# Giving a hand-ordered FFN block to a list scheduler: sigmoid attention and a squared-ReLU FFN on one core

## The chip, the core and the metric

The kernel runs on one core of a Trainium2 chip. The time is the device time of one execution in microseconds (us). The engines are TensorE (PE, with its weight loads shown apart as PEld), VectorE (DVE), ScalarE (ACT), GpSimd (POOL) and SyncE (SP), which issues nearly all transfers. Each engine works through its own instructions in program order and waits for the others by semaphores.

## The reference, cut to what matters

```python
batch, n_heads, seq, head_dim = (8, 12, 448, 64)
n_tokens, d_model, d_ff = (3584, 768, 2048)
...
scores = scale * np.matmul(q, k.transpose(0, 1, 3, 2)) - np.log(S)
attn = 1.0 / (1.0 + np.exp(-scores))
np.matmul(attn, v)
...
h = x @ w_in
r = np.maximum(h, 0.0)
g = s * (r * r) + b
g @ w_out
```

The attention's output, laid out as tokens x 768, is `x`. All inputs are float32; the weights reach the chip as int64 words of doubles and are turned into float32 there.

## The kernel before, in words

**Stages.** The attention runs over 24 quads of heads and stores `x` to DRAM (`xd`). While it runs, DVE and ACT turn the weights into float32 tiles `wf` (one per layer and chunk f of 128 of the 2048 middle features, so 16 chunks per layer). Then comes the *plain block*: token block 0 (512 tokens) goes through the FFN in the ordinary way. The other six token blocks follow in two groups of three by a fast bilinear scheme, whose products need sums of weight blocks. Those sums (`t_0_f_g` for layer 0) are made during the plain block.

**Numbers.** Every operand is split into a rounded part and a remainder (hi on ACT by `copy`, lo on DVE by `sub`), and a product takes three matmuls: hi*hi, hi*lo, lo*hi.

**The plain block.** For each of the 16 chunks, in the order 0, 8, 1, 9, ..., 7, 15:

- `ffn1` (line 804): 18 matmuls into `ph` with the split weight tile `w_0_f`;
- `activate` (line 1262): Relu, Square, Identity, copy on ACT and one subtraction on DVE make `g_f`;
- `ffn2` (line 1272): 18 matmuls into six banks `po` with `w_1_f` and `g_f`. It runs one chunk behind, so PE does ffn1(1), ffn2(0), ffn1(2), ffn2(1), ...; I call each of the 32 pieces of 18 matmuls a *half*.

Beside that, ACT and DVE split each weight tile (`base`, line 546), SP stores the split tile to DRAM (`wd`), from where the products will fetch it (`wu`), and DVE makes the sums `t_0_f_g` (25 additions per f, seven tiles), which are rounded on ACT, subtracted on DVE and stored by SP as well. Two chunks (7 and 15 of layer 0) are still turned into float32 here. Near the end SP loads tokens (`a`) and the first fetched weights (`wu`).

**Where tiles lie.** `w_0_f` and the tiles `t` come from the slots `cx`: eight tiles "c", and five tiles "t" that lie where the attention's buffers were. A slot is free again when its store has landed. `w_1_f` has three buffers (`p2`) and `g` three.

**What sets the order.** In the plain block before, the loop at line 1301 writes the instructions in the order of its statements: per chunk the rounding of the next chunk's weights, half a share of the sums, the activation, the other weight tile, the rest of the share (`rows_until`). Once a queue holds an instruction that has to wait, all behind it wait. The products behind the block are ordered by a list scheduler, class `Planner` (line 247): every operation gets an engine, a duration, what it needs, and a latest time; the scheduler keeps a clock per engine, always issues the operation that can start first, and among several the one that is due first; PE's order is fixed. After the block the scheduler has its own clock set anew, and that code is the same in both kernels.

In the tables below L811 is `ffn1`, L1276 `ffn2`, L543 the rounding of a weight tile, L1265 to L1268 the activation, L487 the rounding of a sum tile, L414 and L417 every addition and subtraction on DVE, L531 and L555 the stores to `wd`, L913 the fetch of `wu`, and L1004 and L1013 the products.

Of the kernel before, what the change touches and what calls it, by code (L numbers as in the profile page):

```python
# [325 lines left out]
def sigmoid_attention_relu2_ffn(  # L326
# [36 lines left out]
    class Slots:  # L363
# [182 lines left out]
    def base(l, f, t=None):  # L546

        t = t or base_hi(l, f)
        sub(t[:, :, 1], wf[l][f], f32(t[:, :, 0]))
# [712 lines left out]
    def activate(f, ph):  # L1262
        g = gp.tile([P, 2, TB], F32R, tag="g", name=f"g_{f}")
        r = rt.tile([P, TB], F32, tag="r", name=f"r_{f}")
        nc.scalar.activation(r, ph, AF.Relu)  # L1265
# [2 lines left out]
        nc.scalar.copy(g[:, 0], r)  # L1268
# [140 lines left out]
```

## Time and profile before

| | before |
|---|---|
| median of 3 runs | 1035.58 us (1034.74 to 1035.64) |
| the profiled execution | 1035.62 us, its span 1033.8 us |
| PE busy | 1018.3 us (98%) |
| DVE, ACT busy | 882.9 us (85%), 716.4 us (69%) |
| plain block on PE | 250.75 to 395.94 us of the span |

The span is the time from the first to the last instruction. PE is busy 98% of it, so only its few gaps and slow stretches can be gained. Rows of the timeline give start, duration, engine, line, output<-input, count, and in brackets the idle time of that engine before the row with what ended it. Names in such rows leave out buffer numbers.

### The profile page before, as it was taken

The page shows a single profiled execution, that of the slowest core. Times are in us where ns is not written, and L with a number is a line of the kernel's source. Part 1 is how long each engine was busy: PE and PEld are TensorE (multiplying, and loading weights), DVE is VectorE, ACT ScalarE, POOL GpSimd, SP SyncE. Part 2 cuts the span into 40 slices and gives each one's busy share as a digit, 9 for nine tenths or more (in the row PEclk, how much of TensorE's full clock was granted, in tenths as well). Part 3 has the DMA queues.
Part 4 walks back from the last instruction along what each step waited for, and adds up shares of the span by engine and source line. Part 5 has one row for each costly group of instructions (what it writes and reads, how often), then busy time and mean ns, then how long its engine had stood idle before and what let it go on. Part 6 is the DMA issues. An engine that isn't in the chain of part 4 may idle for free.

```text
span 1033.8 us, 13813 instructions
## 1 busy us (share of the span) xinstructions
PE 1018.3 (98%) x5194; PEld 761.5 (74%) x5194; DVE 882.9 (85%) x989; ACT 716.4 (69%) x772; POOL 0.2 (0%) x4
## 2 busy tenths in 40 slices
PE   9999999998999999999999999999999999999998
PEld 4545455554776787887887888888888887888887
DVE  6889898997887865999988999899768668999997
ACT  7889998997667656665899964523655889965421
POOL 0000000000000000000000000000000000000000
PEclk9999999999999999999999999999999999999999
DMA  8788999896898899898876666699776666666675
GB/s 335 270 301 303 337 337 387 308 379 233 312 356 295 316 333 401 325 362 303 272 248 186 194 192 196 211 356 311 237 215 195 192 196 190 187 200 188 214 227 185
DMA packets 101073, 278.77 MB, mean 270 GB/s; under 512 B 10000, under 2 KB 23184, under 8 KB 101008
## 3 DMA queue, kind: packets, MB, share of 16 engines
q1 hardware_dynamic: 100720, 277.45, 78.4%
q8 instruction: 41, 0.67, 0.3%
q10 hardware_dynamic: 288, 0.46, 0.1%
q14 instruction: 24, 0.20, 0.1%
HBM read 193.99 MB, written 83.89 MB: 269 GB/s over the span
## 4 chain that ended last, share of the span: by engine, by line
PE 78%; DVE 11%; ACT 5%; DMA 4%; issue 3%; SPq 0%; DVEq 0%; ACTq 0%
PE b L1013 30%; PE b L1004 22%; PE pav L685 10%; PE psc L651 8%; DVE t L417 3%; PE ph L811 2%; PE psc_l L672 2%; PE pav L694 2%; PE po L1276 2%; DVE w L417 1%; DVE r L414 1%; DVE t L414 1%; ACT t L487 1%; ACT w L543 1%; DMA wr<-wr 1%
## 5 line engine op out<-in xcount | busy, mean ns | idle before, releaser
L1004 PE MATMUL b<-o_0h,wu 128*128 128x512 f32 x928 | 287.1, 390 | 0.8 <-DVE r L417 0.7
L1004 PEld LDWEIGHTS b<-o_0h,wu 128*128 128x128 f32 x928 | 174.2, 188 | 38.6 <-DVE r L417 1.6
L1004 PE MATMUL b<-o_0l,wu 128*128 128x512 f32 x464 | 180.8, 390 | 1.0 <-DVE o_0l L417 1.0
L1013 PE MATMUL b<-o_0h,wu 128*128 128x512 f32 x464 | 152.4, 389 | 0.0
L1013 PE MATMUL b<-o_1h,wu 128*128 128x512 f32 x456 | 149.7, 389 | 0.0
L631 ACT ACTIVATE a<-psc,nls 128x896 f32<-128x896 f32 x144 | 132.8, 1009 | 12.2 <-PE psc L651 10.6
L685 PE MATMUL pav<-a,v 128*64 128x448 f32 x576 | 113.8, 543 | 0.0
L414 DVE TENSOR_TENSOR r<-r,b 128x1024 f32<-128x1024 f32 x74 | 89.4, 1218 | 27.1 <-PE b L1004 17.9
L417 DVE TENSOR_TENSOR r<-r,b 128x1024 f32<-128x1024 f32 x66 | 80.2, 1218 | 25.2 <-PE b L1004 16.5
L1004 PEld LDWEIGHTS b<-o_0l,wu 128*128 128x128 f32 x464 | 87.1, 188 | 19.6 <-DVE o_0l L417 1.9
L1013 PEld LDWEIGHTS b<-o_0h,wu 128*128 128x128 f32 x464 | 87.1, 188 | 18.3 <-ACT r L1059 0.3
L1013 PEld LDWEIGHTS b<-o_1h,wu 128*128 128x128 f32 x456 | 85.6, 188 | 17.8
L1013 PE MATMUL b<-o_0l,wu 128*128 128x512 f32 x232 | 90.3, 389 | 0.0
L1013 PE MATMUL b<-o_1l,wu 128*128 128x512 f32 x228 | 88.7, 389 | 0.0
L685 PEld LDWEIGHTS pav<-a,v 128*64 128x64 f32 x576 | 39.1, 137 | 63.8 <-issue 45.1
L487 ACT CAST t<-t 128x768 fp32r<-128x768 f32 (+2 forms) x62 | 44.3, 730 | 53.2 <-DVE t L417 39.3
L954 ACT CAST o_0h<-r 128x1024 fp32r<-128x1024 f32 x26 | 27.1, 1051 | 67.9 <-DVE r L417 40.0
L811 PE MATMUL ph<-x0h,w 128*128 128x512 f32 x192 | 64.5, 404 | 9.1 <-ACT w L543 5.6
L1276 PE MATMUL po<-g,w 128*128 128x512 f32 x288 | 67.7, 389 | 0.0
L1059 ACT ACTIVATE r<-b 128x1024 f32<-128x1024 f32 x46 | 46.4, 1026 | 28.5 <-DVE r L414 13.8
L1276 PEld LDWEIGHTS po<-g,w 128*128 128x128 f32 x288 | 54.1, 188 | 11.2
L417 DVE TENSOR_TENSOR t<-t 128x768 fp32r<-128x768 f32 (+2 forms) x70 | 53.9, 779 | 9.1 <-ACT t L487 8.2
(115 smaller groups left out, 1701.6 us busy)
## 6 DMA issues: line engine op xcount, KB each, us to landing
wu<-wd SPq DMA_DIRECT2D x232, 512.0 KB, 3.6
wd<-t SPq DMA_DIRECT2D x36, 768.0 KB, 4.7
qk<-qk_t SPq DMA_DIRECT2D x23, 896.0 KB, 6.5
st<-w_out SPq DMA_DIRECT2D x16, 768.0 KB, 8.8
st<-w_in SPq DMA_DIRECT2D x16, 768.0 KB, 8.8
wd<-t SPq DMA_DIRECT2D x22, 512.0 KB, 5.4
v<-v_t SPq DMA_DIRECT2D x24, 448.0 KB, 5.2
xd<-xo SPq DMA_DIRECT2D x24, 448.0 KB, 3.4
```

Of the source, the lines that this page charges most:

```text
L414: nc.vector.tensor_tensor(o, x, y, op=ALU.add)
L417: nc.vector.tensor_tensor(o, x, y, op=ALU.subtract)
L487: nc.scalar.copy(ts[g][:, :n, 0], f32(ts[g][:, :n, 1]))
L631: nc.scalar.activation(a, psc[:, :, :S], AF.Sigmoid, bias=nls, scale=SCALE)
L651: nc.tensor.matmul(o[:, j, :S], two[wi][r, i, cols], two[xi][r, i, :S], start=m == 0, stop=m == 2,)
L685: nc.tensor.matmul(pav[r, i, :S], ld_[1][:, 3 * i + c, j, :], a[i, c][:, j, :], start=c == 0, stop=False,)
L811: nc.tensor.matmul(ph, w[:, k, wi, kc * P : (kc + 1) * P], x0[h][xi][:, cc, :], start=m == 0, stop=m == 3 * NCC - 1,)
L954: nc.scalar.copy(hi.t, v.t)
L1004: nc.tensor.matmul(bk[:, j], wt[:, j, wi, c * P : (c + 1) * P], tiles[xi][:, c, :], start=first and m == 0, stop=m == 3 * KC - 1, skip_gro ...
L1013: nc.tensor.matmul(bk[:, e], wt[:, f, wi, e * P : (e + 1) * P], tiles[gi][:, f], start=first and f == 0 and m == 0, stop=p == np_ - 1 and ...
L1059: nc.scalar.activation(v.t, bank_t[b], AF.Copy, scale=-1.0)
L1276: nc.tensor.matmul(pos[e], w[:, k, wi, kc * P : (kc + 1) * P], g[:, gi, :], start=first and i == 0, stop=last and i == 2,)
```

## The change

The loop of the plain block is replaced by operations for a second `Planner` (`plan1`): each half on PE, each rounding, subtraction, activation, each single addition of the weight sums, each store, the two late conversions, the token loads and the first fetches. Each has a duration, needs and a due time. The work left over from the attention (three subtractions and three stores of `t_1_1_g`) becomes such an operation too, instead of coming first. The five "t" slots now come ahead of the free "c" slots. What is computed and how many instructions there are is the same: the instruction lists of both kernels count 3052 rows on PE, 991 on DVE, 776 on ACT and 512 on SP. PE's instructions stand in the same order; those of the attention and of the products keep theirs too.

```diff
-LATE, LATE_AT, LATE_FOR = 2, 2, 4
-ROWS_FOR = 3.5
-TOKENS = (5, 6, 8, 8)
+LATE = 2
+ROWS_DUE = ((10.0, 44.0), (40.0, 72.0), (68.0, 98.0), (90.0, 120.0))
+CONV_DUE = (50.0, 70.0)
+OPEN_DUE = 98.0
+TOKENS = 8
+AHEAD_1, AHEAD_R = 16.0, 40.0
 SUMS_FROM, SUMS_TO = (4, 10), 24
 LATER_SUMS = (2, 3)
 LATER_DUE = ((30.0, 84.0), (86.0, 140.0))
...
-        def more(self, pl, n, tag, when=-99.0):
-            self.free_ += [(when, pl, f"{tag}{i}") for i in range(n)]
+        def more(self, pl, n, tag, when=-99.0, front=False):
+            new = [(when, pl, f"{tag}{i}") for i in range(n)]
+            self.free_ = new + self.free_ if front else self.free_ + new
...
-    ticks(NL, "DVE")
-    for fn in stores:
-        fn()
-    w1 = w1[0]
-    ph0 = ffn1(order[0], w1)
+    ph0 = ffn1(order[0], w1[0])
+    cx.free(w1[0])
     at.close()
...
-    cx.more(pool(blk, "t2", 1), 5, "t")
+    cx.more(pool(blk, "t2", 1), 5, "t", front=True)
...
-    def activate(f, ph):
-        g = gp.tile([P, 2, TB], F32R, tag="g", name=f"g_{f}")
-        r = rt.tile([P, TB], F32, tag="r", name=f"r_{f}")
-        nc.scalar.activation(r, ph, AF.Relu)
-        nc.scalar.activation(r, r, AF.Square)
-        nc.scalar.activation(r, r, AF.Identity, bias=b_sb, scale=s_sb)
-        nc.scalar.copy(g[:, 0], r)
-        sub(g[:, 1], r, f32(g[:, 0]))
-        return g
...
-    held = None
-    w2 = {}
-    row_jobs = [
...
-    cost = sum(j[1] for j in row_jobs[0])
-    before = LATE_AT + LATE * LATE_FOR
-    shares = [(NQ4 - 1) * cost / before] * before + [cost / ROWS_FOR] * (NF - before)
-    row_jobs = collections.deque(j for q_ in row_jobs for j in q_)
-    spent = due = 0.0
-
-    def rows_until(x, roundings=True):
...
+    plan1 = Planner(cx)
+    HALF = 4.09
+    w_t, w_lo, g_t, acts, ffns, ph_t = {}, {}, {}, {}, {}, {0: ph0}
+    row_op, readers, nearly = {}, [], []
+
+    def due(i, l):
+        return max(0.0, (2 * i - 1 + 2 * l) * HALF)
+
+    def weights(l, i):
+        f = order[i]
+        uses = [2 - l]
+
+        def drop(at):
+            uses[0] -= 1
+            if not uses[0]:
+                cx.free(w_t[l, i], at)
+
+        def run_hi(at):
+            w_t[l, i] = base_hi(l, f)
+
+        def keep(at):
+            base_store(l, f, w_t[l, i])
+            if not l:
+                drop(at + 5.0)
+
+        h = plan1.op("ACT", 0.76, [ffns.get((1, i - 3))] if l else [], run_hi, 1 - l, early=AHEAD_1)
+        d = plan1.op("DVE", 0.89, [h], lambda at: base_lo(l, f, w_t[l, i]))
+        k = plan1.op("SP", 0.64 * len(base_rows(l, f)[0]), [d], keep, lag=4.0, late=due(i, l) + 10.0)
+        for r in base_rows(l, f)[0]:
+            row_op[l, r, f % NQ4] = k
+        if f % NP < NP - 1:
...
+    ffns[0, 0] = plan1.op("PE", HALF, [], lambda at: None, late=0.0)
+
+    def first_ffn(i):
+        d, drop = w_lo[0, i]
+
+        def run(at):
+            ph_t[i] = ffn1(order[i], w_t[0, i])
+            drop(at)
+
+        ffns[0, i] = plan1.op("PE", HALF, [d, acts.get(i - 2)], run, late=due(i, 0))
+
+    def second_ffn(i):
+        def run(at):
+            ffn2(w_t[1, i], g_t[i], i == 0, False)
+
+        ffns[1, i] = plan1.op("PE", HALF, [w_lo[1, i][0], g_lo[i]], run, late=due(i, 1))
+
+    g_lo = {}
+
+    def activation(i):
+        f = order[i]
+
+        def run(at):
+            g = g_t[i] = gp.tile([P, 2, TB], F32R, tag="g", name=f"g_{f}")
+            r = r_t[i] = rt.tile([P, TB], F32, tag="r", name=f"r_{f}")
+            nc.scalar.activation(r, ph_t[i], AF.Relu)
+            nc.scalar.activation(r, r, AF.Square)
+            nc.scalar.activation(r, r, AF.Identity, bias=b_sb, scale=s_sb)
+            nc.scalar.copy(g[:, 0], r)
+
+        a = acts[i] = plan1.op("ACT", 2.7, [ffns.get((0, i)), ffns.get((1, i - 3))], run, late=due(i, 1) - 3.6)
+        g_lo[i] = plan1.op("DVE", 0.68, [a], lambda at: sub(g_t[i][:, 1], r_t[i], f32(g_t[i][:, 0])))
...
+    def weight_sums(f):
...
+        chain = [conv.get(f + NP - NQ4), conv.get(f + NF - NQ4)]
...
+        for kind, time, g, fn in jobs:
...
+                his[g] = plan1.op("ACT", 0.04 + 0.24 * len(names[g]), chain, lambda at, fn=fn: fn())
...
+                def run(at, fn=fn, first=tuple(fresh)):
...
+                o = plan1.op("DVE", 0.36, chain, run, len(fresh), early=AHEAD_R)
...
+                o = plan1.op("DVE", time, [his[g]] + chain, lambda at, fn=fn: fn())
...
+                k = plan1.op("SP", 0.64 * len(names[g]), [o], keep, lag=4.0, late=a + (b - a) * spent / total)
...
+    for k, x in enumerate(late):
+        late_conversion(k, *x)
+    for i in range(NF):
+        weights(1, i)
+        if i:
+            weights(0, i)
+            first_ffn(i)
+        activation(i)
+        if i:
+            second_ffn(i - 1)
+    for f in range(NQ4):
+        weight_sums(f)
+
...
+    o = plan1.op("SP", 0.0, readers, opened, late=OPEN_DUE)
+    for k in range(len(FIRST_LOADS)):
+        if k < TOKENS:
+            plan1.op("SP", 1.28, [o], lambda at, k=k: start(FIRST_LOADS[k : k + 1]), late=OPEN_DUE + 2.8 * k)
+    x = None
+    for k in range(AHEAD):
+        _, l, row, p = stream[k]
+        after = [o, x] + [row_op.get((l, row, f)) for f in (2 * p, 2 * p + 1)]
+        x = plan1.op("SP", 1.28, after, lambda at: fetch(), late=OPEN_DUE + 6.0 + 2.8 * k)
+
+    def left(at):
+        ticks(NL, "DVE")
+        for fn in stores:
             fn()
-            spent += w
-
-    for i, f in enumerate(order):
-        if i > NF - 4:
-            a, b = TOKENS[i + 3 - NF : i + 5 - NF]
-            start(FIRST_LOADS[a:b])
-        ph = ffn1(f, w1) if i else ph0
-        if i + 1 < NF:
-            w1 = base(0, order[i + 1])
-        if i == 0:
-            w2[0] = base(1, order[0])
-        rows_until(due + shares[i] / 2, False)
-        g = activate(f, ph)
-        if i + 1 < NF:
-            w2[i + 1] = base(1, order[i + 1])
-        j, stage = divmod(i - LATE_AT, LATE_FOR)
-        if 0 <= j < LATE:
-            if stage == 0:
-                st = cx.tile([P, DM], I64, name=f"st_{late[j][0]}_{late[j][1]}")
-                nc.sync.dma_start(st, w_in[late[j][1]])
-                cv = convert(*late[j], st)
-            elif stage > LATE_FOR - 4:
-                next(cv)
-                if stage == LATE_FOR - 3:
-                    next(cv)
-                if stage == LATE_FOR - 1:
-                    cx.free(st)
-        due += shares[i]
-        rows_until(due)
-        if held:
-            ffn2(*held, i == 1, False)
-        held = (w2[i], g)
-        if i == NF - 4:
-            early.close()
-            roll = pool(ctx, "roll", ROLL, side="right")
-            heap.more(pool(ctx, "h1", 1, side="right"), 12, "r")
-            start(FIRST_LOADS[:TOKENS[0]])
-            for _ in range(4):
-                fetch()
-    assert not row_jobs
-    for _ in range(4, AHEAD):
-        fetch()
+    if (NL, "DVE") in plan:
+        plan1.op("DVE", 2.4, [], left, late=12.0)
+    plan1.full = False
+    plan1.clock.update(PE=0.0, DVE=1.0, ACT=-1.0, SP=1.0)
+    plan1.deadlines()
+    plan1.run()
+    assert not plan
     plan3.clock.update(DVE=-6.0, ACT=-6.0)
     plan3.run(lambda o: o.first)
     plan3.full = False
-    ffn2(*held, False, True)
+    ffn2(w_t[1, NF - 1], g_t[NF - 1], False, True)
```

**PE, from ffn2(9) to ffn1(10).** The piece before, with the semaphores each instruction waits for in brackets:

```order
L1276 MATMUL po_0_2720<-g_9_2931,w_1_9_2867 128x512 [waits Activation_49]
L1276 MATMUL po_0_2720<-g_9_2931,w_1_9_2867 128x512 [waits DVE_49]
L1276 MATMUL po_0_2720<-g_9_2931,w_1_9_2867 128x512
...
L811 MATMUL ph_10_3042<-x0h_0_2539,w_0_10_2988 128x512 [waits Activation_49]
L811 MATMUL ph_10_3042<-x0l_0_2330,w_0_10_2988 128x512
L811 MATMUL ph_10_3042<-x0h_0_2539,w_0_10_2988 128x512 [waits DVE_49]
```

The same place now:

```order
L1269 MATMUL po_0_2714<-g_9_2934,w_1_9_2831 128x512 [waits Activation_49]
L1269 MATMUL po_0_2714<-g_9_2934,w_1_9_2831 128x512 [waits DVE_49]
L1269 MATMUL po_0_2714<-g_9_2934,w_1_9_2831 128x512
...
L818 MATMUL ph_10_3023<-x0h_0_2539,w_0_10_2883 128x512
L818 MATMUL ph_10_3023<-x0l_0_2330,w_0_10_2883 128x512
L818 MATMUL ph_10_3023<-x0h_0_2539,w_0_10_2883 128x512 x2
```

The two waits of `ffn1` on its weight tile are gone: by the time `g_9` was made, the tile `w_0_10` stood ahead of it in ACT's and DVE's order. Before, every one of the 15 later `ffn1` has the pair of waits; now `ffn1` waits for ACT at chunk 8 alone, and for DVE at chunks 8, 9, 5 and 6. `ffn2` waits for its `g` in both.

**ACT, at the start of the block,** before:

```order
L543 CAST w_0_8_2726<-wf_0_8_100 128x3x256 [waits DMAHW4_49,DVE_49,Activation_49]
L543 CAST w_1_0_2730<-wf_1_0_97 128x3x256 [waits PE_49]
L1265 ACTIVATE r_0_2740<-ph_0_2677 128x512 [waits PE_49]
...
L1268 CAST g_0_2739<-r_0_2740 128x512 [waits Activation_49]
L543 CAST w_1_8_2746<-wf_1_8_99 128x3x256
```

and now:

```order
L547 CAST w_1_0_2720<-wf_1_0_97 128x3x256 [waits PE_49,Activation_49]
L547 CAST w_0_8_2722<-wf_0_8_100 128x3x256 [waits DMAHW6_49,DMAHW7_49,DMAHW3_49,DVE_49]
L547 CAST w_1_8_2724<-wf_1_8_99 128x3x256 [waits Activation_49]
L547 CAST w_0_1_2727<-wf_0_1_102 128x3x256
L547 CAST w_1_1_2731<-wf_1_1_101 128x3x256 [waits Activation_49]
L547 CAST w_0_9_2735<-wf_0_9_104 128x3x256
L1335 ACTIVATE r_0_2758<-ph_0_2671 128x512 [waits PE_49]
...
L1338 CAST g_0_2757<-r_0_2758 128x512 [waits Activation_49]
```

The rounding of `w_0_8` used to wait for the store of a leftover tile `t_1_1_5` (DMAHW4); it now takes a "t" slot, over the attention's buffers, and waits for the last store of `x` among others (DMAHW3; the next lines show that store). Four more roundings stand ahead of the first activation.

**SP, at the end of the block,** now (DMAHW3 is also the semaphore of the store of `x` at the start, whose row comes first here):

```order
L709 DMA xd_7_90<-xo_7_2_2668 128x896 [waits DMAHW3_49,DVE_49]
L563 DMA wd_1_0_93<-w_1_0_2720 128x512 [waits DMAHW4_49,DVE_49]
...
L1399 DMA wd_0_1_92<-t_0_3_5_3621 128x3x512 [waits DMAHW7_49,DVE_49]
...
L563 DMA wd_1_1_94<-w_1_14_3531 128x2x512 [waits DMAHW5_49]
L563 DMA wd_0_1_92<-w_0_7_3505 128x2x512 [waits DMAHW6_49]
L916 DMA wu_6_3785<-wd_0_0_91 128x1024 [waits DMAHW7_49]
L563 DMA wd_1_1_94<-w_1_7_3619 128x2x512 [waits DMAHW0_49]
L563 DMA wd_0_1_92<-w_0_15_3595 128x2x512 [waits DMAHW1_49]
L563 DMA wd_1_1_94<-w_1_15_3748 128x2x512 [waits DMAHW2_49,DVE_49]
L916 DMA wu_7_3970<-wd_0_1_92 128x1024 [waits DMAHW3_49,PE_49]
```

and before:

```order
L555 DMA wd_0_1_92<-w_0_7_3642 128x2x512 [waits DMAHW6_49,DVE_49]
L555 DMA wd_1_1_94<-w_1_7_3654 128x2x512 [waits DMAHW7_49,DVE_49]
...
L555 DMA wd_0_1_92<-w_0_15_3707 128x2x512 [waits DMAHW6_49,DVE_49]
L555 DMA wd_1_1_94<-w_1_15_3718 128x2x512 [waits DMAHW7_49,DVE_49]
L913 DMA wu_4_3784<-wd_0_0_91 128x1024 [waits DMAHW0_49]
L913 DMA wu_5_3786<-wd_0_1_92 128x1024 [waits DMAHW1_49]
L913 DMA wu_6_3788<-wd_0_0_91 128x1024 [waits DMAHW2_49]
L913 DMA wu_7_3970<-wd_0_1_92 128x1024 [waits DMAHW3_49,PE_49]
```

Five more stores of weight sums and of `w_1_14` now stand behind the first token loads, and the fetches `wu_4` to `wu_6` ahead of the last stores. The store of `w_1_15` is the last store of the block in both.

More of the change, by code (lines that the diff above doesn't have):

```diff
@@ L544, in base_hi, with base_lo, base_rows, base_store @@
         return t
-    def base(l, f, t=None):
-        t = t or base_hi(l, f)
+    def base_lo(l, f, t):
         sub(t[:, :, 1], wf[l][f], f32(t[:, :, 0]))
-        part, f = divmod(f, NQ4)
-        name = (lambda k: f"{part}{k}") if l else (lambda k: f"{k}{part}")
-        thirds = [k for k in range(3) if name(k) in ROWS[l]]
+    def base_rows(l, f):
+        part = f // NQ4
+        names = [f"{part}{k}" if l else f"{k}{part}" for k in range(3)]
+        return [x for x in names if x in ROWS[l]], [k for k in range(3) if names[k] in ROWS[l]]
+    def base_store(l, f, t):
+        names, thirds = base_rows(l, f)
+        f %= NQ4
         step = thirds[-1] - thirds[0] if len(thirds) == 2 else 1
-        row, n = ROWS[l].index(name(thirds[0])), len(thirds)
+        row, n = ROWS[l].index(names[0]), len(thirds)
         nc.sync.dma_start(
@@ L558, in base @@
         )
-        kept.update((l, name(k), f) for k in thirds)
-        return t
+        kept.update((l, x, f) for x in names)
     def load_tokens(dst, t, c0, n):
@@ L839, in sigmoid_attention_relu2_ffn @@
     at_step(NL - 2, "ACT", 8, lambda: w1.append(base_hi(0, 0)))
-    at_step(NL - 1, "DVE", 1, lambda: base(0, 0, w1[0]))
+    at_step(NL - 1, "DVE", 1, lambda: (base_lo(0, 0, w1[0]), base_store(0, 0, w1[0])))
     parts_dve(*quads[0], loaded[0], [(0, slice(S)), (1, slice(S)), (0, slice(S + 2 * P, NX)), (1, slice(S, NX))])
@@ new lines, in sigmoid_attention_relu2_ffn, with late_conversion, load, last @@
+    r_t, conv = {}, {}
+    def late_conversion(k, l, f):
+        v = {}
+        end = CONV_DUE[k]
+        def load(at):
+            v["st"] = cx.tile([P, DM], I64, name=f"st_{l}_{f}")
+            nc.sync.dma_start(v["st"], w_in[f])
+            v["cv"] = convert(l, f, v["st"])
+        def last(at):
+            next(v["cv"])
+            cx.free(v["st"], at)
+        step = lambda at: next(v["cv"])
+        o = plan1.op("SP", 2.0, [], load, 1, early=20.0, lag=6.0)
+        o = plan1.op("DVE", 0.57, [o], step)
+        o = plan1.op("ACT", 0.95, [o], step)
+        o = plan1.op("DVE", 1.52, [o], step)
+        conv[f] = plan1.op("DVE", 1.9, [o], last, late=end)
@@ new lines, in sigmoid_attention_relu2_ffn, with opened @@
+    for k, x in enumerate(late):
[10 more added lines that the diff above has]
+        weight_sums(f)
+    def opened(at):
+        nonlocal roll
+        early.close()
+        roll = pool(ctx, "roll", ROLL, side="right")
+        heap.more(pool(ctx, "h1", 1, side="right"), 12, "r")
+    o = plan1.op("SP", 0.0, readers, opened, late=OPEN_DUE)
@@ new lines, in sigmoid_attention_relu2_ffn @@
+    for k in range(len(FIRST_LOADS)):
[9 more added lines that the diff above has]
+        for fn in stores:
+            fn()
+        stores.clear()
```

41 lines of the change are left out of this document (34 added, 7 removed).

## The prediction

> **What bounds the kernel now.** I read the shares of the chain that ended last, then the waits of PE, then busy times by stretches of the plain block.
>
> ```profile
> PE 78%; DVE 11%; ACT 5%; DMA 4%; issue 3%; SPq 0%; DVEq 0%; ACTq 0%
> PE ph L811 <- ACT w L543: 5.6, 4, 4.0
> PE ph L811 <- DVE w L417: 3.5, 6, 1.3
> core 0: us, PE busy (x) PEld busy (x) DVE busy (x) ACT busy (x) POOL busy (x), PEclk, DMA share, GB/s
> 254.00:266.00 12.00, 8.01 (x28) 5.66 (x27) 8.52 (x16) 5.60 (x8) 0.00 (x0) 0.86 0.80 308
> 266.00:376.00 110.00, 104.88 (x451) 83.22 (x450) 92.79 (x167) 73.53 (x106) 0.00 (x0) 1.00 0.85 319
> 376.00:396.00 20.00, 20.00 (x90) 16.58 (x89) 10.20 (x12) 11.38 (x18) 0.00 (x0) 1.00 1.05 389
> 396.00:480.00 84.00, 82.93 (x364) 67.70 (x363) 74.00 (x97) 51.07 (x60) 0.00 (x0) 1.00 0.96 358
> ```
>
> The first row says that PE is the bound over the whole run. A wait row gives the total, the number of waits and the longest: in the plain block PE waits 9.1 us for weight tiles, 4.0 of it once. No row says that `po` waits for `g`. The windows show that DVE and ACT are busy less than PE in the middle of the block, so they have room; what makes PE wait is the order of their work.
>
> How much can be gained is read from the starts of the halves on PE:
>
> ```profile
> 250.75 0.50 PE L811 MATMUL ph<-x0h,w 128*128 128x512 f32 x1
> 259.14 0.55 PE L811 MATMUL ph<-x0h,w 128*128 128x512 f32 x1 [3.97 <-ACT w L543]
> 265.19 4.24 PE L1276 MATMUL po<-g,w 128*128 128x512 f32 x18
> 269.27 0.39 PE L811 MATMUL ph<-x0h,w 128*128 128x512 f32 x1
> 273.35 4.24 PE L1276 MATMUL po<-g,w 128*128 128x512 f32 x18
> 277.43 0.39 PE L811 MATMUL ph<-x0h,w 128*128 128x512 f32 x1
> 335.79 4.24 PE L1276 MATMUL po<-g,w 128*128 128x512 f32 x18
> 345.62 4.24 PE L1276 MATMUL po<-g,w 128*128 128x512 f32 x18
> 355.14 4.24 PE L1276 MATMUL po<-g,w 128*128 128x512 f32 x18
> 395.94 0.39 PE L1004 MATMUL b<-o_0h,wu 128*128 128x512 f32 x1
> ```
>
> A half without a wait takes 277.43 - 273.35 = 4.08 us, so 32 halves need 130.6 us. The block lasts 395.94 - 250.75 = 145.19 us: 14.6 us are lost. The first three halves take 269.27 - 250.75 = 18.52 us instead of 12.24 (6.28 lost). The other 29 take 126.67 instead of 118.32 (8.35 lost). Those 8.35 us lie between 281 and 355 us: 335.79 to 345.62 to 355.14 are 9.83 and 9.52 us for two halves that need 8.16. The wait rows show about 5 of the 8.35; a delay shorter than the drawn length of a matmul (0.39 us, at a pitch of 4.08/18 = 0.23) doesn't appear as idle time.
>
> **The change part by part.** Nothing is added or removed; each cost is one of place.
>
> *Start of the block.* What holds the second `ffn1` today:
>
> ```profile
> 253.77 0.32 SPq L702 DMA_DIRECT2D xd<-xo  x1
> DMA to landing us min/median/max: 2.5/2.5/2.5
> 254.67 3.49 DMA wd<-t
> 258.26 1.56 ACT L543 CAST w<-wf 128x768 fp32r<-128x768 f32 x2 [7.31 <-DMA wd<-t]
> 259.73 0.59 ACT L1265 ACTIVATE r<-ph 128x512 f32<-128x512 f32 x1
> 261.86 0.62 ACT L1268 CAST g<-r 128x512 fp32r<-128x512 f32 x1
> 262.38 0.83 ACT L543 CAST w<-wf 128x768 fp32r<-128x768 f32 x1
> 263.12 0.83 ACT L487 CAST t<-t 128x768 fp32r<-128x768 f32 x1
> 262.51 0.69 DVE L417 TENSOR_TENSOR g<-r,g 128x512 fp32r<-128x512 f32 x1
> ```
>
> The rounding of `w_0_8` waits for the store of a leftover sum tile, issued at 254.67 and landed at 258.16; ACT sits idle 7.31 us before it, and the rounding starts 0.10 us after the landing. In the new order it waits for the last store of `x` instead: issued 253.77, plus 2.5 to landing, plus 0.10, gives 256.37. `ffn1` follows the rounding by 259.14 - 258.26 = 0.88, so it starts at 257.25. But four roundings now stand between this one and the activation of chunk 0; with a pitch of 263.12 - 262.38 = 0.74 us, the activation starts at 256.37 + 5 x 0.74 = 260.07, which is 0.34 later than today. From there to the rounding of `g_0` is 261.86 - 259.73 = 2.13, DVE's subtraction starts 262.51 - 261.86 = 0.65 later and takes 0.69: `g_0` is whole at 263.54. `ffn1(8)` took 265.19 - 259.14 = 6.05 us at the lowered clock (0.86 in the window's row); even at that length it ends at 263.30, so `g_0`'s remainder decides, and it is needed by the second of the 18 matmuls: `ffn2(0)` ends at 263.54 + 17 x 0.227 = 267.40 instead of 269.27. **The start gains 1.9 us**, and no more: most of the wait on the weight becomes hidden by, or moves into, the making of `g_0`. The bounds are 0 (if the rounding is held by a tile that I take to be free, the store at 254.67 above all) and 18.52 - 12.24 = 6.3.
>
> *Middle of the block.* `ffn1` waits for a weight tile because its rounding stands behind the activation and a share of the sums. In the new order the tile stands ahead of the `g` that the preceding `ffn2` already waits for, so the wait is gone by order. What may replace it is a wait of `ffn2` for `g`:
>
> ```profile
> DVE t L417 <- ACT t L487: 8.2, 11, 1.4
> DVE g L417 <- ACT g L1268: 5.2, 6, 1.0
> DVE w L417 <- ACT w L543: 2.9, 3, 1.3
> L417 DVE TENSOR_TENSOR g<-r,g x13: 683/692/694, 270.7 to 375.3; 128x512 fp32r<-128x512 f32 x13
> 387.98 0.60 ACT L1265 ACTIVATE r<-ph 128x512 f32<-128x512 f32 x1 [4.66 <-PE ph L811]
> 390.78 0.69 DVE L417 TENSOR_TENSOR g<-r,g 128x512 fp32r<-128x512 f32 x1 [6.47 <-ACT g L1268]
> ```
>
> The last two rows are an undisturbed activation: from the end of `ffn1` (0.02 before 387.98) to the finished `g` at 391.47 are 3.5 us. `g_i` is needed two halves after its `ffn1`, 8.16 us, so 4.7 us of delay are free. DVE has 92.79 us of work in the window with 13 activations: 7.1 us for each, against 8.16 that PE allows; counting the instructions between two `g` in the new order (shares of the sums are now cut into single additions) gives 7.0 to 8.1 by the same durations, where the old order had up to 10. ACT's 73.53 us are 5.7 each. So DVE fits, barely, and **the middle gains 8.35 us**. The bounds: 0 if none of it goes, 8.35 if all; a DVE that also waits for ACT is a rival below.
>
> *Leftover subtractions and stores, and the slots.* They move behind the first activations; their DVE work is the same and lies in the slack above: nothing.
>
> *Token loads and stores at the end.* Five stores now stand behind the first token loads in SP's queue. PE doesn't wait for tokens in the block, but the first products do:
>
> ```profile
> 392.95 8.72 DMA wd<-w
> 401.69 10.04 DMA wr<-wr
> 402.83 1.23 DVE L417 TENSOR_TENSOR s_None<-a,s_None 128x1024 f32<-128x1024 f32 x1 [5.60 <-DMA wd<-w]
> 411.75 0.42 DVE L417 TENSOR_TENSOR t<-wr 128x256 f32<-128x256 f32 x1 [2.96 <-DMA wr<-wr]
> 413.37 0.50 PE L1004 MATMUL b<-o_0l,wu 128*128 128x512 f32 x1 [0.38 <-DVE o_0l L417]
> 479.62 0.50 PE L1004 MATMUL b<-o_0l,wu 128*128 128x512 f32 x1 [0.65 <-DVE o_0l L417]
> DMA packets 25989, 48.76 MB, mean 332 GB/s; under 512 B 1359, under 2 KB 5455, under 8 KB 25981
> ```
>
> The last store of the block lands at 401.67, the load of `wr` starts then, and the operand that DVE makes behind it holds PE 0.38 us at 413.37: the landing was 0.38 late. If the block ends 10.25 us earlier, the landing must come by 401.67 - 0.38 - 10.25 = 391.0, or PE waits there for each us beyond. The last row is the traffic from 254.7 to that landing: 48.76 MB at 332 GB/s. This is the unknown of the change. At the mean rate of today the landing stays where it is; but today's rate has pauses in which nothing was ready to be moved. In the windows, the rate over the share of busy DMA engines is 319/0.85 = 375 and 389/1.05 = 370 GB/s; at 372 the landing is at 254.7 + 131 = 385.8, before 391.0. I take no cost. The bounds are 0.4 us gained (that wait gone too) and, at the 319 GB/s of the middle window, a landing at 407.5 and 16.5 us lost.
>
> The Trainium skill ("DMA: Bandwidth & Descriptors", section "Where 436 GB/s comes from") says that for transfers between HBM and SBUF the HBM side binds, at about 358 GB/s for a core. By an estimate from that figure the landing would be at 254.7 + 136.2 = 390.9, just in time with no slack left, which would make the last rival below likelier than I hold it. The window from 376 to 396 moved 389 GB/s, so this trace doesn't bear that figure out as a ceiling.
>
> **Sum**: 1.87 + 8.35 = 10.2 us. The profiled execution took 1035.62 us (span 1033.8 and 1.8 around it), practically the median of 1035.58. 1035.62 - 10.2 = **1025.4 us**, with the block's end at 385.7.
>
> **The rivals.**
>
> *The queues still wait in order.* The windows count busy time only. In the window DVE also waited 8.2 + 5.2 + 2.9 = 16.3 us for roundings on ACT. If these waits stay, a unit costs DVE (92.79 + 16.3)/13 = 8.39 us, 0.23 more than PE's 8.16; over 13 units that is 3.0 us, and PE waits for `g`: 1028.4, or 1027 to 1030 as the free 4.7 us absorb a part. For it: the pairs rounding and subtraction are all still there, and a unit of 8.1 leaves no room. Against it: the new order issues roundings well ahead of their subtractions, and much of the waiting today is idle time of an engine with nothing due.
>
> *The stall only moves.* The roundings stand early in the order, but the tiles they write are not free: a slot comes free when a store has landed, so ACT waits in front of an activation, and `g` is late by what `ffn1` waited before. Only the start's 1.9 us would remain: 1033.7. For it: the one such wait that the profile shows, 7.31 us. Against it: it is the leftover store's, and the order no longer has that wait there.
>
> *Slower, by the store queue.* The loads of tokens stand ahead of stores in SP's queue, which issues in order, so the last store lands late and the products, with PE's order fixed, wait at the place of today's 0.38 us. Each us behind 391.0 costs one. The point from which the whole change loses is a landing at 401.2, a mean of 48.76 MB/146.5 us = 333 GB/s; at 319 the time is 1025.4 + 16.5 = 1042. For it: the last 20 us of the block already run at a DMA share of 1.05, and the whole stretch at 332. Against it: with earlier production the pauses fill.
>
> **How the numbers follow.** The forecast has 0.60, with a range of its own of 1024.0 to 1027. The waits on DVE have 0.20 (1028.4), the moved stall 0.08 (1033.7), the store queue 0.12, more than half of it slower than before, as a rate between 333 and 355 GB/s costs only a part of the gain. 0.2% (2 us) is about what a measurement of this kernel tells from no change. Faster beyond that: 0.60 + 0.20 + 0.04 = 0.84. Within it: the moved stall and a queue close to its break-even, 0.09. Slower: 0.07. The range reaches from 1024.0 (the sum with the 0.38 and the 0.65 us of the two later waits gone as well, and a little of the start) over the second case to 1031.5, a store queue that takes half the gain.
>
> **What would show it right or wrong.** In the changed profile the wait before the second `ffn1` ends at 257.2 and the first `po` begins near 263.3; the rows of `ph` waiting for `w` shrink to that one and a few short ones; `po` has no row of waiting for `g`; the first product starts at 385.7; the DVE row with `DMA wd<-w` begins by 392; and the waits after that stay under 1 us. A wait of `po` on `g` of several us would mean the first rival; idle time of ACT ahead of roundings that wait for DMA the second; a wait of `b` on an operand around 403 the third. The forecast is wrong at its root if the halves in the middle don't fall to 8.16 us for two.

## The result and the profile after

The changed kernel's median is 1078.95 us over 4 runs (1024.46 to 2077.31), because two of them were disturbed (1130.52 at a granted clock of 0.851, and 2077.31) beside 1024.46 and 1027.38. A second measurement of the same kernel gave **1025.37 us** (1024.98 to 1025.94), beside 1035.43 for the kernel before; ratio 0.9901, interval 0.9886 to 0.9917. The first measurement gave a ratio of 0.9908 (0.9883 to 0.9934). The forecast was 1025.4. All rows below are of the second measurement.

The profiled execution took 1025.94 us, its span 1024.2. The waits of PE (total, number, longest):

```profile
PE ph L818 <- ACT w L547: 2.0, 1, 2.0
PE b L1007 <- DVE o_0l L421: 1.1, 1, 1.1
PE po L1269 <- ACT g L1338: 0.7, 1, 0.7
PE ph L818 <- DVE w L421: 0.3, 1, 0.3
PE po L1269 <- DVE g L421: 0.2, 1, 0.2
```

L818 and L1269 are `ffn1` and `ffn2` now, L547 the rounding of a weight tile, L1007 a product. 9.1 us of waits for weight tiles have become 2.3, all at the start; `po` waits 0.9 us for `g`, which it didn't before. The timeline of PE:

```profile
251.42 0.50 PE L818 MATMUL ph<-x0h,w 128*128 128x512 f32 x1
257.84 0.50 PE L818 MATMUL ph<-x0h,w 128*128 128x512 f32 x1 [2.00 <-ACT w L547]
263.44 0.49 PE L1269 MATMUL po<-g,w 128*128 128x512 f32 x1 [0.69 <-ACT g L1338]
264.16 4.15 PE L1269 MATMUL po<-g,w 128*128 128x512 f32 x17 [0.23 <-DVE g L421]
268.15 0.39 PE L818 MATMUL ph<-x0h,w 128*128 128x512 f32 x1
321.19 4.24 PE L1269 MATMUL po<-g,w 128*128 128x512 f32 x18
329.35 4.24 PE L1269 MATMUL po<-g,w 128*128 128x512 f32 x18
386.47 0.39 PE L1007 MATMUL b<-o_0h,wu 128*128 128x512 f32 x1
```

The block begins 0.67 us later than in the profile before (the attention differs by that much from run to run), so lengths are compared. The block takes 386.47 - 251.42 = 135.05 us instead of 145.19. The first three halves take 268.15 - 251.42 = 16.73 instead of 18.52, the other 29 take 118.32 instead of 126.67: exactly 29 x 4.08. The windows of the start, the rest of the block, the products, and two inside the block:

```profile
core 0: us, PE busy (x) PEld busy (x) DVE busy (x) ACT busy (x) POOL busy (x), PEclk, DMA share, GB/s
252.00:264.00 12.00, 8.98 (x36) 6.22 (x34) 8.96 (x11) 7.37 (x12) 0.00 (x0) 1.00 0.53 203
264.00:386.00 122.00, 121.84 (x537) 100.90 (x538) 103.55 (x184) 83.38 (x118) 0.00 (x0) 1.00 0.99 373
386.00:470.00 84.00, 82.78 (x365) 67.89 (x363) 74.16 (x97) 50.65 (x61) 0.00 (x0) 1.00 0.92 340
290.00:355.00 65.00, 65.00 (x289) 53.81 (x288) 61.31 (x112) 46.87 (x67) 0.00 (x0) 1.00 0.94 360
355.00:376.00 21.00, 21.00 (x94) 17.41 (x93) 12.18 (x20) 12.20 (x18) 0.00 (x0) 1.00 1.05 381
```

Two things are new. The transfers' share over 122 us is 0.99, at 373 GB/s, so most of the pauses are gone; in its fullest stretches this share reads 1.05, and one pause is left (0.79 from 310 to 330 us). And DVE is busy 61.31 of 65 us (94%) up to 355 and 12.18 of 21 behind that; the kernel before did 54.82 us of work in the same 65 (its row is in the next section).

### The profile page after: what moved, and what is told of

Same layout as the page of the kernel before. It is cut to its first block, busy times and chain, and to the rows that moved or that the text cites. A ratio compares the mean times of both kernels' runs of the same rounds, so it can differ in the third digit from the quotient of the medians.

```text
span 1128.7 us, 13810 instructions
## 1 busy us (share of the span) xinstructions
PE 1123.0 (99%) x5194; PEld 779.5 (69%) x5194; DVE 885.4 (78%) x989; ACT 721.8 (64%) x772; POOL 0.2 (0%) x4
## 4 chain that ended last, share of the span: by engine, by line
PE 97%; DMA 1%; ACT 1%; DVE 0%; issue 0%; SPq 0%; ACTq 0%; DVEq 0%
PE b L1007 31%; PE b L1016 31%; PE pav L692 11%; PE psc L658 8%; PE po L1269 6%; PE ph L818 6%; PE psc_l L679 2%; PE pav L701 2%; DMA qk<-qk_t 0%; ACT w L547 0%; PE o L1030 0%; DMA wd<-w 0%; DMA xd<-xo 0%; ACT t L491 0%; DVE x0l L421 0%
## 5 line engine op out<-in xcount | busy, mean ns | idle before, releaser
L1007 PE MATMUL b<-o_0h,wu 128*128 128x512 f32 x928 | 309.7, 417 | 0.0
L1007 PEld LDWEIGHTS b<-o_0h,wu 128*128 128x128 f32 x928 | 177.9, 192 | 55.5 <-DVE r L421 0.6
L1007 PE MATMUL b<-o_0l,wu 128*128 128x512 f32 x464 | 193.9, 418 | 0.0
L1016 PE MATMUL b<-o_0h,wu 128*128 128x512 f32 x464 | 164.3, 416 | 0.0
L1016 PE MATMUL b<-o_1h,wu 128*128 128x512 f32 x456 | 161.5, 416 | 0.0
L692 PE MATMUL pav<-a,v 128*64 128x448 f32 x576 | 131.3, 610 | 0.0
L1016 PEld LDWEIGHTS b<-o_0h,wu 128*128 128x128 f32 x464 | 89.2, 192 | 27.6
L1007 PEld LDWEIGHTS b<-o_0l,wu 128*128 128x128 f32 x464 | 89.3, 193 | 26.7
L1016 PE MATMUL b<-o_0l,wu 128*128 128x512 f32 x232 | 97.1, 419 | 0.0
L1016 PE MATMUL b<-o_1l,wu 128*128 128x512 f32 x228 | 95.4, 419 | 0.0
L1269 PE MATMUL po<-g,w 128*128 128x512 f32 x288 | 75.1, 418 | 0.6 <-ACT g L1338 0.3
L818 PE MATMUL ph<-x0h,w 128*128 128x512 f32 x192 | 66.9, 418 | 1.0 <-ACT w L547 0.8
L1269 PEld LDWEIGHTS po<-g,w 128*128 128x128 f32 x288 | 55.3, 192 | 18.0 <-ACT g L1338 0.8
L1136 ACT ACTIVATE r<-r,b_sb,s_sb 128x1024 f32<-128x1024 f32 x48 | 59.6, 1241 | 1.0
```

The costliest lines, as they stand in the source:

```text
L692: nc.tensor.matmul(pav[r, i, :S], ld_[1][:, 3 * i + c, j, :], a[i, c][:, j, :], start=c == 0, stop=False,)
L818: nc.tensor.matmul(ph, w[:, k, wi, kc * P : (kc + 1) * P], x0[h][xi][:, cc, :], start=m == 0, stop=m == 3 * NCC - 1,)
L1007: nc.tensor.matmul(bk[:, j], wt[:, j, wi, c * P : (c + 1) * P], tiles[xi][:, c, :], start=first and m == 0, stop=m == 3 * KC - 1, skip_gro ...
L1016: nc.tensor.matmul(bk[:, e], wt[:, f, wi, e * P : (e + 1) * P], tiles[gi][:, f], start=first and f == 0 and m == 0, stop=p == np_ - 1 and ...
L1136: nc.scalar.activation(v.t, v.t, AF.Identity, bias=b_sb, scale=s_sb)
L1269: nc.tensor.matmul(pos[e], w[:, k, wi, kc * P : (kc + 1) * P], g[:, gi, :], start=first and i == 0, stop=last and i == 2,)
```

## The experiments

**The changed kernel again**, without an edit; its result and rows are the ones above.

> The changed kernel once more, for a profile at the full clock. Theory (the order removes PE's waits for weight tiles): 1025.4 us, the first product at 385.7, two halves in the middle take 8.16 us, the last store lands before 391. Rival (waits of DVE for ACT stay): 1028.4 with waits of po for g in the middle. Rival (store queue): the first product at 385.7 but waits of b between 396 and 412.

The theory's numbers came: 385.7 is 134.95 us behind the block's start, 135.05 were measured, and no pair of halves in the middle takes more than 8.16 us. The last store landed after 391, which is taken up below.

**The start.** Two edits to it were tried apart: the place of the slots alone in the old kernel, and the old start in the new one.

```diff
-    cx.more(pool(blk, "t2", 1), 5, "t")
+    cx.free_ = [(-99.0, pl_, f"t{i}") for pl_ in [pool(blk, "t2", 1)] for i in range(5)] + cx.free_
```

> The kernel before with one edit: the five t slots come first, so that the rounding of w_0_8 waits for the last store of x and not for the leftover store; the old loop writes the order. Theory (the first wait is the slot's): ffn1(8) starts at 257.3 instead of 259.1 and the kernel gains 1.9 us, 1033.7; the middle keeps its 8.35 us. Rival (slots were the cause of the middle's waits too): 1025 to 1028. Rival (the wait at the start has another cause): 1035.6.

Measured: 1033.96 us (1032.76 to 1035.21), ratio 0.9985 (0.9976 to 0.9993). Its first three halves take 16.89 us, the others 126.36: only the start gains (1.63 us), as in theory.

```diff
-    cx.more(pool(blk, "t2", 1), 5, "t", front=True)
+    cx.more(pool(blk, "t2", 1), 5, "t")
...
-        plan1.op("DVE", 2.4, [], left, late=12.0)
+        left(0.0)
```

> The changed kernel with the two edits of its start undone: the leftover subtractions and stores come first again and the t slots last; the scheduler still orders the rest. The rounding of w_0_8 then takes the slot of w_0_0, which is free when ffn1(0) ends at 255.0. Theory (the gain of the middle is the scheduler's alone, the start's hangs on the slot only): ffn1(8) starts at 256.1, g_0 is whole at 262.3, 1024 to 1025. Rival (the late leftover work and the early t slots are what lets the scheduler gain): 1027.3 or more, the start back at 259.1.

Measured: 1024.41 us (1023.31 to 1025.39), ratio 0.9893 (0.988 to 0.9907). The start takes 16.29 us, the other 29 halves 118.32 again. So the middle's gain doesn't need the new start. Nor is the new start the better one: in the old order of slots `w_0_8` gets the place of `w_0_0`, and its rounding starts 4.46 us into the block (behind `ffn1(0)`), where in the changed kernel it starts 5.53 us in (behind the store of `x`). The two kernels' times overlap, so this difference is read from the traces alone.

That was carried further: `w_0_8` in one of the buffers of `w_1`, `w_1_8` in a slot instead, and the true time of the "t" slots told to the scheduler.

```diff
-        if l:
+        if (l == 1) != (f == 8):
             t = p2.tile(shape, F32R, tag="w", name=f"w_{l}_{f}")
...
-    cx.more(pool(blk, "t2", 1), 5, "t", front=True)
+    cx.more(pool(blk, "t2", 1), 5, "t", when=5.6, front=True)
...
+        slot = (l == 1) == (f == 8)
-        uses = [2 - l]
+        uses = [2]
...
-            if not uses[0]:
+            if not uses[0] and slot:
                 cx.free(w_t[l, i], at)
...
-            if not l:
-                drop(at + 5.0)
+            drop(at + 5.0)
...
-        h = plan1.op("ACT", 0.76, [ffns.get((1, i - 3))] if l else [], run_hi, 1 - l, early=AHEAD_1)
+        h = plan1.op("ACT", 0.76, [ffns.get((1, i - 3))] if l else [], run_hi, int(slot), early=AHEAD_1)
...
             ffn2(w_t[1, i], g_t[i], i == 0, False)
+            w_lo[1, i][1](at)
```

> The changed kernel with the tiles of the start placed elsewhere: w_0_8 takes one of the three buffers of w_1, w_1_8 takes a slot instead, and the scheduler is told that the t slots come free 5.6 us into the block. No rounding ahead of the first activation waits for the store of x any more. On PE the first three halves should take 12.6 us instead of 16.9, and the first product start 4 us earlier in the block. Theory A (PE's halves alone set the end): 1025.4 - 4.2 = 1021.2. Theory B (the transfers are the next bound: the share of busy DMA engines was 0.99 in the changed kernel's block): the last store lands as late as before, PE waits for the operand behind it, and 1023 to 1025 remain.

Measured: **1022.22 us** (1021.29 to 1022.87), ratio 0.9869 (0.9855 to 0.9882): faster than both kernels, though by 1.3% and 0.3% only. The start takes 13.43 us of an ideal 12.24; the block is 3.30 us shorter than the changed kernel's, the time 3.15. Theory B is not borne out: the last store's place moved with the block (the DVE row that waits for it starts 6.60 us behind the first product, 6.93 in the changed kernel): with tiles made earlier the transfers fill earlier too (a share of 0.73 from 252 to 264 us, 0.53 in the changed kernel). Theory A's 1021.2 was 1 us too good, as the start kept 1.2 us.

**The middle: is it the place of the weight tiles?** In the old loop, each `w_0` tile one chunk earlier:

```diff
-        ph = ffn1(f, w1) if i else ph0
-        if i + 1 < NF:
-            w1 = base(0, order[i + 1])
+        ph = ffn1(f, w1.pop(0)) if i else ph0
+        if i == 0:
+            w1 = [base(0, order[1])]
+        elif i + 2 < NF:
+            w1.append(base(0, order[i + 2]))
...
+        if i == 0:
+            w1.append(base(0, order[2]))
         if i + 1 < NF:
             w2[i + 1] = base(1, order[i + 1])
```

> The kernel before, its loop kept, with one edit: each w_0 tile is rounded and subtracted one chunk earlier than it was, so that by the order only the second and third ffn1 wait for weights. Theory (the middle's loss is only the place of these roundings): 8.35 us go, 1027.3. Rival (the coarse shares of sums between two g, up to 10 us on DVE, take over): waits of po for g, part of the gain, 1030 to 1033.

Measured: 1035.48 us (1035.26 to 1036.75), ratio 1.0 (0.9991 to 1.0009): nothing gained. The waits of PE in this kernel:

```profile
PE ph L811 <- ACT w L543: 4.0, 1, 4.0
PE po L1276 <- ACT g L1268: 1.9, 2, 1.1
PE po L1276 <- DVE g L417: 1.8, 6, 0.6
```

The weight tiles are in time, and PE waits for `g` in their place. The 29 halves take 124.66 us, so 6.34 of the 8.35 us are still lost. What PE waits for by name need not be what is late: if all that ACT and DVE make is late together, PE names whichever comes last. My theory fell here, and the rival's figure (1030 to 1033) was too kind as well: the 2.0 us that the middle gained went to a longer start (19.40 us) and to waits behind the block (one of 0.85 us that wasn't there). The longer start need not come from the edit: a kernel further down, with the start as it was before, shows 19.39 us at the same granted clock (0.78 from 252 to 264 us, where the kernel before had 0.86).

The waits of ACT and DVE for each other at sum tiles, weight tiles and `g` in the window 290 to 355, where most of the loss lies, of the kernel before:

```profile
ACT t L487 <- DVE t L417: 15.7, 6, 4.4
DVE t L417 <- ACT t L487: 4.5, 5, 1.4
ACT t L487 <- DVE t L414: 4.4, 1, 4.4
DVE w L417 <- ACT w L543: 2.6, 2, 1.3
DVE g L417 <- ACT g L1268: 2.5, 3, 1.0
290.00:355.00 65.00, 59.88 (x253) 46.24 (x252) 54.82 (x97) 41.47 (x59) 0.00 (x0) 1.00 0.84 321
```

and of the changed one:

```profile
ACT t L491 <- DVE t L421: 2.7, 2, 1.5
DVE g L421 <- ACT g L1338: 2.6, 7, 0.7
ACT t L491 <- DVE t L418: 1.3, 2, 0.9
DVE t L421 <- ACT t L491: 0.4, 1, 0.4
```

Before, ACT stood 20.1 us at roundings of sum tiles until DVE had finished the sum, and DVE stood 7.1 us at the subtractions of `t` and `w` until ACT had rounded. In the old loop a subtraction stands directly behind its rounding. Where ACT could not run ahead, such a pair costs DVE about the length of the rounding: 4.5 us at 5 of the 15 sum tiles of this window, 0.9 us each, beside 0.83 us for a rounding. The next two kernels move only the subtractions away from their roundings. First, with the tiles ahead:

```diff
-            w1.append(base(0, order[i + 2]))
+            w1.append(base_hi(0, order[i + 2]))
...
         rows_until(due + shares[i] / 2, False)
+        if i and i + 2 < NF:
+            base(0, order[i + 2], w1[-1])
...
-            w2[i + 1] = base(1, order[i + 1])
+            w2[i + 1] = base_hi(1, order[i + 1])
...
         rows_until(due)
+        if i + 1 < NF:
+            base(1, order[i + 1], w2[i + 1])
...
-    row_jobs = collections.deque(j for q_ in row_jobs for j in q_)
+    row_jobs = list(enumerate(j for q_ in row_jobs for j in q_))
+    row_jobs.sort(key=lambda x: x[0] + (5.5 if x[1][0] == "lo" else 0.0))
+    row_jobs = collections.deque(j for _, j in row_jobs)
```

> The kernel with tiles a chunk ahead once more, still in the old loop, and now each subtraction stands some instructions behind the rounding that it needs: those of the sum tiles five jobs later, those of w_0 and w_1 behind half a share of sums. Theory C (DVE was full in its order: 54.8 us of work and 9.6 us of waits for ACT in the 65 us from 290 to 355 of the kernel before, so the waits, not the work, held g or w): the 6.3 us that the middle still lost go for the most part, 1029 to 1031. Rival (the lumps of a share, up to 10 us between two g, hold it whatever the waits): 1034 to 1036.

Measured: 1027.30 us (1027.23 to 1027.75), ratio 0.9917 (0.9904 to 0.9931), better than the 1029 to 1031 of theory C. The 29 halves take 118.32 us, not one wait left among them. Then without the tiles ahead, on the kernel before (the edits of `w2` and of `row_jobs` alone):

```diff
-            w2[i + 1] = base(1, order[i + 1])
+            w2[i + 1] = base_hi(1, order[i + 1])
...
         rows_until(due)
+        if i + 1 < NF:
+            base(1, order[i + 1], w2[i + 1])
...
-    row_jobs = collections.deque(j for q_ in row_jobs for j in q_)
+    row_jobs = list(enumerate(j for q_ in row_jobs for j in q_))
+    row_jobs.sort(key=lambda x: x[0] + (5.5 if x[1][0] == "lo" else 0.0))
+    row_jobs = collections.deque(j for _, j in row_jobs)
```

> The kernel before with its w_0 tiles where they were, and only the subtractions of the sum tiles (five jobs) and of w_1 (behind the rest of the share) moved behind their roundings. Theory C alone (DVE's waits for ACT are the whole loss): the middle goes to 8.16 us for two halves, 1027 to 1028. Rival (the place of the w_0 roundings matters too, once the waits are gone): a part of the 8.35 us stays, 1029 to 1033.

Measured: 1027.20 us (1025.73 to 1027.66), ratio 0.9914 (0.99 to 0.9927); again 118.32 us for the 29 halves. The first of them and the first product, its two largest waits of ACT and DVE for each other between 290 and 355, and that window:

```profile
269.33 0.39 PE L811 MATMUL ph<-x0h,w 128*128 128x512 f32 x1
387.65 0.39 PE L1004 MATMUL b<-o_0h,wu 128*128 128x512 f32 x1
ACT t L487 <- DVE t L417: 10.3, 6, 2.8
DVE g L417 <- ACT g L1268: 5.1, 6, 1.4
290.00:355.00 65.00, 65.00 (x288) 53.82 (x287) 59.42 (x109) 45.62 (x65) 0.00 (x0) 1.00 0.93 353
```

DVE no longer waits for ACT at `t` or `w`, and does 59.42 us of work there instead of 54.82. Six lines in the old loop give the whole gain of the middle; the place of the `w_0` tiles doesn't matter for it. Its rival (that the place matters too) falls. Which of the two moves, that of the sum tiles or that of `w_1`, does more was not run. With the slots' 1.63 us at the start these lines add up to 9.98 of the 10.14 us by which the change shortens the block, without a scheduler; the two were not run together.

**The grain of the sums.** The change also cuts the sums into single additions. Here they are given in runs of one to five:

```diff
             elif kind == "sum":
-                def run(at, fn=fn, first=tuple(fresh)):
-                    for x in first:
-                        x()
-                    fn()
-
-                o = plan1.op("DVE", 0.36, chain, run, len(fresh), early=AHEAD_R)
-                if f < NQ4 - 1:
-                    readers.append(o)
-                fresh, chain = [], [o]
+                acc.append((tuple(fresh), fn))
+                fresh = []
...
+                o = plan1.op("DVE", 0.36 * len(fns), chain, run, sum(len(x) for x, _ in fns), early=AHEAD_R)
```

> The changed kernel, but the additions of the weight sums go to the scheduler in runs of one to five, as they stand between two roundings, and not one by one. Theory C (what counts is that no subtraction waits for its rounding and that shares and conversions are spread): 1025 to 1026. Rival (single additions are what keeps g in time): two halves in the middle over 8.16 us, 1028 to 1032.

Measured: 1025.65 us (1024.87 to 1025.75), ratio 0.9901 (0.9885 to 0.9916), 118.32 us once more. The fine grain isn't needed.

**What bounds the block next.** Four of the `w_0` stores issued twice, in the changed kernel:

```diff
-            base_store(l, f, w_t[l, i])
+            for _ in range(2 if not l and i in (4, 6, 8, 10) else 1):
+                base_store(l, f, w_t[l, i])
```

> The changed kernel with four of the w_0 stores, 0.52 MB each, issued twice in the first half of the block: 2.1 MB more, 5.6 us at the 373 GB/s that the block moved. Theory B (the block's transfers are at their bound and the last store is just in time): the last store lands 5.6 us later, the operand behind it holds PE at 397, 1030.5. Theory A (the queue has room): 1025.4 to 1026.

Measured: 1035.35 us (1034.36 to 1036.81), 9.98 more than the changed kernel's 1025.37. Theory B's direction holds, but it gave 5 us and twice that came. The operand behind the last store, the product that waits, the next 14 us of this kernel, and the two longest waits of DVE and ACT for stores between 290 and 355:

```profile
401.99 1.23 DVE L421 TENSOR_TENSOR s_None<-a,s_None 128x1024 f32<-128x1024 f32 x1 [13.27 <-DMA wd<-w]
406.19 0.79 PE L1007 MATMUL b<-o_0h,wu 128*128 128x512 f32 x1 [7.70 <-ACT r L1062]
406.00:420.00 14.00, 13.81 (x49) 11.17 (x50) 13.12 (x22) 12.12 (x15) 0.00 (x0) 0.78 0.60 212
DVE t L418 <- DMA wd<-t: 5.5, 3, 3.1
ACT w L547 <- DMA wd<-t: 3.2, 1, 3.2
```

The block is only 0.26 us longer; the products wait 7.70 us, and behind that wait the granted clock is 0.78 for 14 us, which is worth up to 3 us and covers the 2 us that are left. The DVE row begins 14.55 us behind the first product (387.44), against 6.93 in the changed kernel, 7.6 later for 2.1 MB, where 5.6 were expected. The last two rows, which the changed kernel doesn't have, point to a reason: a slot comes free when its store has landed, so doubled stores also hold back DVE and ACT, and with them later stores. The same two rows in the changed kernel, with the store:

```profile
382.42 10.86 DMA wd<-w
393.40 1.23 DVE L421 TENSOR_TENSOR s_None<-a,s_None 128x1024 f32<-128x1024 f32 x1 [5.65 <-DMA wd<-w]
397.12 0.98 PE L1007 MATMUL b<-o_0h,wu 128*128 128x512 f32 x2
```

A pair of such matmuls takes 0.62 us elsewhere, so 0.36 us of waiting is hidden in the last row: here the last store is just too late already, and from there each us costs about one (7.6 us later, 7.3 us more of waiting). It was so in the kernel before as well. Its last two stores of weight tiles, and the pair of matmuls at the same place:

```profile
L555 SPq DMA_DIRECT2D wd<-w x2: 650/993/1336, 393.0 to 394.4; - x2
DMA to landing us min/median/max: 8.3/8.5/8.7
406.60 0.93 PE L1004 MATMUL b<-o_0h,wu 128*128 128x512 f32 x2
```

There 0.31 us were hidden, and the DVE row began 6.89 us behind the first product. So in the change the last store moved with the end of the block, and this wait costs 0.05 us more than before.

The same stores twice in the kernel before (`base` issues them there):

```diff
-        nc.sync.dma_start(
+        for _ in range(2 if not l and f in (2, 3) and not part or not l and f in (0, 1) and part == 1 else 1):
+          nc.sync.dma_start(
```

> The kernel before with the same four w_0 stores issued twice, 2.1 MB more. Theory B (the kernel before had pauses in its transfers, a share of 0.85, the changed one has none, 0.97 to 0.99): the pauses take them up, 1035.6 to 1037. Rival (any store more in the block costs its time): 1041 or more.

Measured: 1037.08 us (1035.63 to 1038.03) against 1035.89, ratio 1.001 (1.0002 to 1.0019): 1.2 us, not 10. In the profiled execution the later 29 halves take 126.42 us, no longer than before; the block's 0.62 us more lie in its start (19.39 us), which ends ahead of the first doubled store and had a granted clock of 0.78. So the pauses took the doubled stores up.

And DVE's room in the changed kernel, by doing each subtraction of a `w_0` tile twice:

```diff
-        d = plan1.op("DVE", 0.89, [h], lambda at: base_lo(l, f, w_t[l, i]))
+        d = plan1.op("DVE", 0.89, [h], lambda at: [base_lo(l, f, w_t[l, i]) for _ in range(1 + (l == 0))])
```

> The changed kernel, with the subtraction of each w_0 tile done twice (15 times 0.87 = 13 us more on DVE, which was busy 103.6 of 122 us there); the order isn't told of it. Theory (DVE has 15% of room and g has 4.7 us of slack): at most 1 us more, 1025.4 to 1026.4. Rival (waits in order eat the room): PE waits for g in the middle, up to 13 us, 1030 to 1038.

Measured: 1036.34 us (1035.53 to 1039.07), 11.0 more for 13 us of work, within the rival's range. The block is 4.84 us longer (2.1 at the start, 2.7 in the middle), and then the products wait, for the same store:

```profile
290.00:355.00 65.00, 64.55 (x286) 53.11 (x285) 64.12 (x111) 44.75 (x64) 0.00 (x0) 1.00 0.85 325
402.03 1.22 DVE L421 TENSOR_TENSOR s_None<-a,s_None 128x1024 f32<-128x1024 f32 x1 [9.31 <-DMA wd<-w]
406.23 0.80 PE L1007 MATMUL b<-o_0h,wu 128*128 128x512 f32 x1 [3.74 <-ACT r L1062]
```

So the room that I read from the windows isn't there: what DVE makes has to be stored before the block ends, and up to 355 us it is 94% busy already. Here it is busy 64.12 of 65 us, and the transfers, with a share of 0.85 there (0.94 in the changed kernel), fall behind. Not all of the 11 us is DVE's work: the granted clock was 0.78 from 252 to 264 us (1.00 in the changed kernel) and 0.78 again from 406 to 420, behind the wait.

## Why the prediction was right, and where its reasons were not

- **Sum**: 10.2 us, of which 10.14 appeared in the block (1.79 at the start, 8.35 in the middle). The time, 1025.37, is the forecast's. One slip: half the gain, which is to give the range's upper end, would be 1030.5 and not 1031.5.
- **Start**: every step held. Shifted by the 0.67 us of this run, the second `ffn1` was due at 257.92 and came at 257.84; the remainder of `g_0` was due at 264.21, and the second matmul of `ffn2(0)` ran at 264.16. One thing differed: `ffn1(8)` ran at the full clock (1.00 in the window, 0.86 before) and was over 0.7 us before `g_0`, so that `g_0` alone decided. The edit of the slots alone gave the same start (16.89 us).
- **Middle**: the size was right and the step's reason wrong. I wrote that `ffn1` waits "because its rounding stands behind the activation and a share of the sums" and that the wait "is gone by order". Putting the tiles earlier alone gained nothing; PE then waited for `g`. The loss was what I held for a rival of the changed kernel, waits of DVE and ACT for each other in order: (92.79 + 16.3)/13 = 8.39 us for a unit, over PE's 8.16, was a description of the kernel *before*, where DVE's work and these waits fill 109.1 of the window's 110 us. In the scheduler's order DVE waits for the rounding of a sum tile for 0.4 us in all from 290 to 355 (4.5 before), and the kernel with only the subtractions moved shows that this is enough. So the 8.35 us came by another way than the one I gave; that the size was right is in part luck.
- **DVE's room**: "7.1 us for each, against 8.16" took the load as even. In the changed kernel it isn't: 61.31 of 65 us up to 355, then 12.18 of 21. DVE did fit, but 13 us more cost 11.
- **Last store**: I took no cost, and 0.05 us came, but by luck, since both numbers behind it were wrong. The landing at 401.67 is that of the store before the last one; the last one (`w_1_15`) landed at 394.4 + 8.3 = 402.7, and what stands behind it is the operand `s` (the DVE row at 402.83) and not the product at 413.37. PE is not held if the DVE row of `s` begins within about 6.6 us of the first product (6.89 - 0.31 before, 6.93 - 0.36 now): by 393.0 here, not 391.0. And the store landed at 393.3, not 385.8, as 50.78 MB had been moved by then, at a mean of 366 GB/s, where I had 48.76 MB at 372. The load of `wr`, which I took for the path, was now issued at 389.81, ahead of that landing. The third rival's mechanism is real, and the changed kernel stands at its edge: 2.1 MB more bring it to 1035.35. Nor did the DVE row begin by 392, as I had asked: it began at 393.40, or 392.7 less the 0.67 us of this run.
- **The figure of the Trainium skill** that I weighed ("DMA: Bandwidth & Descriptors", section "Where 436 GB/s comes from", about 358 GB/s for a core) is no ceiling here: 373 GB/s over 122 us. By it I would have held the last rival likelier and the landing at 390.9, nearer to the 393.3 measured than mine, but by accident: the bytes were more, and the rate was not that low (366 GB/s).
- **Waits behind the block**: 1.1 us at one product (0.65 before), a little over the 1 us that I allowed; the 0.38 at 413.37 is gone.

## What to carry to other kernels

When one engine rounds and another subtracts the rounded part, put work of a few instructions between the two on the second engine. Directly behind each other, such a pair can cost the second engine the first one's duration (0.9 us at each sum tile that DVE waited for here). If that fills the second engine, PE waits for whichever operand comes last, and moving that operand alone only renames the wait. Count an engine's load as busy time plus its own waits, up to the last time at which its output is still of use, not over the whole stage. When a stage gets shorter, it still has the same bytes to move: compare their share before and after, and find the first consumer of the last store.

## What was not expected of the hardware

After a wait PE often ran slower for a while. Behind the 7.70 us wait the granted clock was 0.78 over 14 us, and at the start of the kernel before, with a wait of 3.97 us, 0.86 over 12; single matmuls there took 0.63 us, 0.40 at the full clock. The changed kernel's start, with a wait of 2.00, kept 1.00. But the same wait gave 0.86 from 252 to 264 us in the kernel with doubled stores, 0.86 in the one with sums in runs and 0.78 in the one with doubled subtractions, and the kernel with the old start had 0.86 with waits of only 0.92 and 0.77. So neither a threshold nor the length of the wait alone follows from these runs.
